# The layout in DRAM of a layer's output and its gradient: by partition and row block instead of row by row

## The chip, the cores and the metric

The kernel runs on one core of a Trainium2 chip. The time is the device time of one execution in microseconds. Before the change three runs took 749.44, 753.18 and 754.14 us; the median is 753.18.

## What is computed

A block with two branches and a gate, forward and backward. For u of 2048 x 448 (L x D) and the output gradient G:

```python
g = sigmoid((u * gate_w).sum(-1, keepdims=True))
a = ssm_conv(u, A, B, C, log_dt) + u * Dskip      # a long convolution, by FFT in the reference
r = relu(u @ w1 + b1)                             # w1: 448 x 1792
b = (r * r) @ w2 + b2                             # w2: 1792 x 448
out = g * a + (1 - g) * b
```

and the gradients of out with respect to u and to all parameters. Everything is bfloat16. For the dense branch (b) the backward pass needs dB = (1 - g) * G, dw2 = (r*r)^T dB, dh = 2 r * (dB w2^T), dw1 = u^T dh, and the part dh w1^T of u's gradient. r and dh have 2048 x 1792 elements, 7.3 MB each.

## The kernel before

The core has 128 partitions. r and dh are held turned: the 1792 columns lie in 14 groups of 128 (`FT = 14`, the index j), one column a partition, with the 2048 rows along the partition. They don't fit into the core's memory beside the convolution's tables, so each group is written to DRAM when it is made (`rT_d` and `dhT_d`, 1792 x 2048 elements, row after row) and read back later. Eight *row blocks* of 256 rows each cut the 2048 rows the other way.

The dense branch is one generator, `dense()`, of 190 or so steps with a hand-written cost for each; the convolution's 14 chunks are the frame, and the steps are put between its parts:

- *First layer* (some 70 to 260 us), for each j: `hidden` makes r's group j by TensorE (L661, L664) and ACT (L676) and stores it (L681 on POOL's queue; the last three, which come while `hold` is set, are deferred and go out on SP's queue, L679). TensorE turns it (L688), ACT squares it (L689), and a product over the rows gives dw2 (L697, stored by L704).
- *Second layer* (some 265 to 450 us), for each j: `load_r` reads group j of r back (L772 whole, or L775 in two halves where j is a multiple of three), three groups ahead; `grad_h` makes dB w2^T (L661, L664), ACT doubles it (L784), and a *gate* on DVE multiplies it by r (L789). The result, dh's group j, is stored by L794 on SP's queue and turned and multiplied by u for dw1.
- *Two projections* (`project`, some 450 to 605 us, the last of it at 630): for each of the eight row blocks, in the order 0, 4, 1, 5, ..., all 14 groups of a block of r are loaded (`load_rows2`, L881 on SP's queue), squared by ACT (L893, the first block L858) and multiplied by w2 (L905); then the same with dh and w1 turned. w1 is turned on its way by a DMA transpose in seven pieces (`load_w1t`, L925, SP's queue). Four buffers take the blocks in turn; three of them get a block in one transfer, the fourth has two pieces of memory and gets it in two transfers of seven groups.

The convolution's chunk c has a table Y that DVE builds in five steps (`build_y`: L1018, L1019, L1021). TensorE multiplies it at once (`kgen`, L1082), and four DMA transposes on SP's queue turn it (`load_yt`, L1106) for chunk c's backward products. The next chunk's first write to Y is a DVE copy, `seeds_y` (L1059), so it waits for those four transposes. The order of the parts in a chunk is written out:

```python
PERIOD = """YS SA Z0 D R Y0 Y1 D Z1 Y2 D R Y3 Z2 D NX Y4 D Z3 KM KO LY WD P0 D P1 D X0 FY0 S FY1 FY2 X1 D R X2 D""".split()
```

YS is `seeds_y`, Y0 to Y4 build Y, KM is `kgen`, LY issues the four transposes, P0 and P1 are DVE's products of the chunk before (L1159, L1161), D lets the dense branch take steps up to a share of its cost. While `hold` is set, transfers that the dense branch wants on SP's queue (r's loads, dh's stores, row blocks, w1's pieces, w2) are put into a list, `held`, by `defer`; R, and LY after its own four transposes, issue what is in the list (`release`). Each engine and each queue runs what it is given strictly in that order.

`rows_of(tensor, j)` at L647 is the address pattern of one group; `load_r` has a pattern of its own for half a group, and `load_rows2` one for a row block. These three are what the diff touches.

Of the kernel before, what the change touches and what calls it, by code (L numbers as in the profile page):

```python
# [19 lines left out]
P = 128  # L20
L, D, N, F = 2048, 448, 256, 1792
LT = L // P
FT = F // P
# [296 lines left out]
def kernel(ctx, tc, A_u, A_A_re, A_A_im, A_B_re, A_B_im, A_C_re, A_C_im, A_log_dt, A_Dskip,  # L320
# [3 lines left out]
    nc = tc.nc  # L324
# [6 lines left out]
    def dscr(name, n, dt=bf16):  # L331
        return nc.dram_tensor(name, (n,), dt, kind="Internal")
# [9 lines left out]
    rT_d = dscr("rT_d", F * L)  # L342
    dhT_d = dscr("dhT_d", F * L)
# [282 lines left out]
    BK = dict(h=("N2", "N3"), t="S", a="X", p=("N0", "N1", "N2", "N3"))  # L626
    dbt, r3, dhs, held, pend = [], [], [], [], []
    hold = False
    db1 = const.tile([P, FT], bf16, name="db1")
    acc = {}  # L630
    rcur, rts = {}, [(b, -1) for b in rt]
# [13 lines left out]
            release()  # L645

    def rows_of(tensor, j):  # L647
        return bass.AP(tensor=tensor, offset=j * P * L, ap=[[L, P], [1, L]])

    def load_w1(jp):  # L650
        b = w1b[jp % 2]
# [15 lines left out]
    def hidden(j, half):  # L667
        pss = wide(half, w1b[j // 2 % 2][:, :, P * (j % 2):P * (j % 2) + P], lambda lb: UT[:, :, 512 * lb:512 * lb + 512])
        if half == 0:
            rcur[j], prev = rts.pop(0)  # L670
            rts.append((rcur[j], j))
            force(prev)
        r = rcur[j]
        for k in range(2):
            lb = 2 * half + k
            S.activation(r[:, 512 * lb:512 * lb + 512], pss[k][:], ACT.Relu, bias=b1_f[:, j:j + 1])  # L676
        if half == 1:
            if hold:
                held.append((j, lambda: nc.sync.dma_start(rows_of(rT_d, j), r)))  # L679
            else:  # L680
                G_.dma_start(rows_of(rT_d, j), r)  # L681
            if j % 2 == 1 and j // 2 + 2 < HP:
                load_w1(j // 2 + 2)
# [37 lines left out]
    def first_layer():  # L721
# [6 lines left out]
        for j in range(FT):  # L728
            if j + 1 < FT:
                hidden(j + 1, 0)  # L730
            turn(j, 0, rcur[j], ACT.Square)
            yield
            if j > 0:
                mul_1(j - 1, 1)
                if j == FT - 3:
                    load_w2(0)
                if j == FT - 1:
                    defer(j, load_u)
                    if r3:
                        load_r(0)  # L740
                        acc["r"] = 1
                yield
            if j + 1 < FT:
                hidden(j + 1, 1)
            turn(j, 1, rcur[j], ACT.Square)
            if j == FT - 2:
                load_w2(1)
            yield
            mul_1(j, 0)
            yield  # L750
            if j in (1, 2):
                for k in range(4):
                    turn_db(4 * j - 4 + k)
                    yield
# [15 lines left out]
    def load_r(j):  # L770
        if j % 3 > 0:
            nc.sync.dma_start(rt[j % 3 - 1], rows_of(rT_d, j))  # L772
        else:
            for h in range(2):
                nc.sync.dma_start(r3[0][h], bass.AP(tensor=rT_d, offset=j * P * L + 1024 * h, ap=[[L, P], [1, 1024]]))  # L775

    def grad_h(j, half):

        force(j - 3)
        pss = wide(half, w2T[j % 2], lambda lb: dbt[lb])  # L780
        dh = dhs[j % 3]
        for k in range(2):
            lb = 2 * half + k
            S.mul(dh[:, 512 * lb:512 * lb + 512], pss[k][:], 2.0)  # L784

        def gate():
            force(j - 3)
            d = dh[:, 1024 * half:1024 * half + 1024]
            V.tensor_tensor(out=d, in0=d, in1=r3[j % 3][half], op=ALU.mult)  # L789
            if half == 1:  # L790
                def go():
                    if j + 3 < FT:
                        load_r(j + 3)
                    nc.sync.dma_start(rows_of(dhT_d, j), dh)  # L794
                defer(j, go)
        pend.append(gate)
# [23 lines left out]
    def second_layer():  # L820

        release()
        for j in range(acc.get("r", 0), 3):
            load_r(j)
# [6 lines left out]
        for j in range(FT):  # L831
            gates()
            if j in (3, 5, 7, 9):
                k0, k1 = (4 * (j // 2) - 4, min(4 * (j // 2), FT))
                defer(j, lambda k0=k0, k1=k1: nc.sync.dma_start(w2n[:, k0:k1], bass.AP(tensor=B_w2.tensor, offset=B_w2.offset + k0 * P * D, ap=[[D, P], [P * D, k1 - k0], [1, D]])))
            if j == FT - 1:
                load_rows2(0)
            if j + 1 < FT:
                grad_h(j + 1, 0)
            turn(j, 0, dhs[j % 3], ACT.Copy)  # L840
            yield
            if j > 0:
                mul_2(j - 1, 1)
            if j + 2 < FT:
                turn_w2(j + 2)
            yield
            gates()
            if j + 1 < FT:
                grad_h(j + 1, 1)
            turn(j, 1, dhs[j % 3], ACT.Copy)  # L850
            yield
            mul_2(j, 0)
            if j > 0:
                turn_back(j - 1)
            yield
# [4 lines left out]
        yield  # L860
        turn_back(FT - 1)
        load_rows2(1)
        defer(98, lambda: load_rows2(2))
        defer(99, lambda: load_rows2(3))
        defer(99, lambda: load_w1t(0))

    PO = [0, 4, 1, 5, 2, 6, 3, 7]
# [5 lines left out]
    def slot_of(n):  # L873

        return pring[0 if n == 15 else n % 4]

    def load_rows2(n):
        bs = slot_of(n)
        m = FT // len(bs)
        for i, b in enumerate(bs):  # L880
            nc.sync.dma_start(b, bass.AP(tensor=rT_d if n < 8 else dhT_d, offset=256 * PO[n % 8] + i * m * P * L, ap=[[L, P], [P * L, m], [1, 256]]))  # L881

    nbk = 0

# [401 lines left out]
    r3 = [[KW[:, 6144:7168], Pt[:, 6144:7168]]] + [[rt[i][:, 0:1024], rt[i][:, 1024:2048]] for i in range(2)]  # L1286
# [105 lines left out]
    i = PERIOD.index("KM")  # L1392
# [303 lines left out]
```

## Time and profile before

The profiled execution took 752.95 us; its span, from the first instruction to the last, is 751.1 us.

| | us | share of the span | instructions |
|---|---|---|---|
| PE (TensorE matmul) | 621.1 | 83% | 8556 |
| DVE (VectorE) | 564.7 | 75% | 932 |
| ACT (ScalarE) | 512.1 | 68% | 873 |
| POOL (GpSimd) | 171.6 | 23% | 296 |

The core moved 177.77 MB in 197,115 DMA packets. SP's queue (q1) had 173,823 of them, 113.11 MB; POOL's (q0) 15,632 and 44.48 MB; ACT's (q10) 7,568 and 18.88 MB. The transfers that touch the two tensors, from the page's list of DMA issues, "us" being the median from issue to landing where the trace has it:

| transfer | line and queue | count | KB each | pieces in DRAM | us |
|---|---|---|---|---|---|
| r's group to rT_d | L681, POOL | 11 | 512 | 4,096 B | 3.0 |
| r's group to rT_d, deferred | L679, SP | 3 | 512 | 4,096 B | |
| r's group back | L772, SP | 9 | 512 | 4,096 B | 4.7 |
| half a group back | L775, SP | 10 | 256 | 2,048 B | 8.8 and 3.1 |
| dh's group to dhT_d | L794, SP | 14 | 512 | 4,096 B | 5.9 |
| row block | L881, SP | 12 | 896 | 512 B | 6.3 to 9.6 |
| half the groups of a row block | L881, SP | 8 | 448 | 512 B | 8.1 |

How to read it: PE, DVE, ACT and POOL are the engines, SP the queue engine that issues most DMAs; "SPq" and "POOLq" are the instructions by which a queue issues. L12 is line 12 of the kernel. An idle time before an instruction stands in brackets with what ended it; a wait for several things is put down to the one that came last by the profile. "PE psN<-D,U" is a matmul that writes psN and reads D and U, buffer numbers left out. A DMA's "share of 16 engines" adds up its packets' times, so it can pass 100% where packets overlap.

### The profile page before, as it was taken

What the parts mean: (1) busy time and instruction counts of PE and PEld (TensorE: products, weight loads), DVE (VectorE), ACT (ScalarE), POOL (GpSimd) and SP (SyncE); (2) the same over time, 40 slices, a digit from 0 to 9 for tenths busy, and PEclk for the clock granted to TensorE, in tenths of its full rate; (3) what the DMA queues carried; (4) which work ended last, traced back from release to release, by engine and by line L of the source; (5) the groups of instructions that cost most, each with busy time, mean ns of one, the idle gap of its engine ahead of it and who ended that gap; (6) DMA issues with size and microseconds to landing.
All of it is one profiled execution on the core that took longest, in us unless ns stands there. A gap on an engine that the chain in (4) does not pass through costs nothing.

```text
span 751.1 us, 20458 instructions
## 1 busy us (share of the span) xinstructions
PE 621.1 (83%) x8556; PEld 337.4 (45%) x8597; DVE 564.7 (75%) x932; ACT 512.1 (68%) x873; POOL 171.6 (23%) x296
## 2 busy tenths in 40 slices
PE   5947968779999787999989997888969978687666
PEld 2412323323346453665665664555545664433111
DVE  1495586675698456899898997988699877959473
ACT  2895958587887576778777777777634535597555
POOL 2251112111263220211201201110100332411543
PEclk9887967879999899999999999999989988799758
DMA  9997586827773997997997989999999966998995
GB/s 211 220 280 243 195 294 240 291 103 285 283 263 134 249 256 214 200 249 203 219 209 216 240 137 240 244 198 245 218 186 234 276 165 199 389 333 297 333 327 147
DMA packets 197115, 177.77 MB, mean 237 GB/s; under 512 B 121534, under 2 KB 174039, under 8 KB 196895
## 3 DMA queue, kind: packets, MB, share of 16 engines
q1 hardware_dynamic: 173823, 113.11, 61.9%
q0 software_dynamic: 15632, 44.48, 19.3%
q10 hardware_dynamic: 7568, 18.88, 6.7%
q8 instruction: 67, 1.10, 0.6%
q14 instruction: 25, 0.20, 0.1%
HBM read 83.95 MB, written 64.32 MB: 197 GB/s over the span
## 4 chain that ended last, share of the span: by engine, by line
PE 28%; DMA 12%; DVE 10%; ACT 7%; issue 7%; POOL 1%; SPq 0%; POOLq 0%; ACTq 0%; DVEq 0%
PE psN L905 5%; PE psS L1176 5%; DMA R<-Y 3%; PE psN L661 3%; PE psX L1082 3%; PE psN L697 3%; DVE Y L1021 2%; DVE Y L1018 2%; DVE F L1019 2%; DMA U<-in_A_u_dram 2%; DMA S<-in_B_w_dram 2%; DMA hd<-F 2%; PE psN L296 1%; PE psF L1144 1%; ACT P L1150 1%
## 5 line engine op out<-in xcount | busy, mean ns | idle before, releaser
L697 PEld LDWEIGHTS <-U 128*128 128x128 bf16 x448 | 40.6, 99 | 42.4 <-issue 12.1
L1150 ACT CAST P<-psF 128x1024 bf16<-128x1024 f32 x52 | 53.1, 1021 | 7.0 <-PE psF L1144 6.8
L1018 DVE TENSOR_TENSOR Y<-Y,F 128x1024 bf16<-128x1024 bf16 (+3 forms) x70 | 48.0, 686 | 2.7
L661 PEld LDWEIGHTS <-S 128*128 128x128 bf16 x336 | 30.2, 101 | 44.1 <-issue 18.5
L1021 DVE TENSOR_TENSOR Y<-Y,F 128x1024 bf16<-128x1024 bf16 (+3 forms) x70 | 48.1, 687 | 2.4
L697 PE MATMUL psN<-S,U 128*128 128x449 bf16 x224 | 47.8, 355 | 0.2 <-issue 0.2
L661 PE MATMUL psN<-S 128*128 128x512 bf16 x153 | 46.3, 415 | 1.9 <-issue 1.0
L1019 DVE TENSOR_TENSOR F<-Y,F 128x1024 bf16<-128x1024 bf16 (+3 forms) x70 | 47.2, 674 | 0.0
L697 PE MATMUL psX<-D,U 128*128 128x448 bf16 x160 | 37.3, 370 | 2.0 <-ACT D L703 2.0
L689 ACT ACTIVATE U<-psN 128x1024 bf16<-128x1024 bf16 x35 | 36.1, 1032 | 1.5 <-PE psN L688 1.5
L1183 POOL DMA_DIRECT2D s_d<-st x28 | 14.0, 506 | 97.6 <-ACT st L1181 97.6
L905 PEld LDWEIGHTS <-U 128*128 128x128 bf16 x252 | 24.2, 100 | 24.7 <-issue 4.7
L676 ACT ACTIVATE U<-psN,b_f 128x512 bf16<-128x512 f32 x48 | 31.0, 688 | 6.0 <-PE psN L664 4.3
L1144 PEld LDWEIGHTS <-R 41*128 41x128 bf16 x1792 | 27.0, 93 | 17.8 <-issue 15.0
L1144 PE MATMUL psF<-S,R 41*128 41x32 bf16 x1664 | 29.4, 174 | 5.9 <-ACT P L1150 5.9
L661 PE MATMUL psN<-K,S 128*128 128x512 bf16 x100 | 27.6, 391 | 5.6 <-issue 3.2
L905 PE MATMUL psN<-S,U 128*128 128x448 bf16 x140 | 29.0, 358 | 1.8 <-DMA S<-in_B_w_dram 1.8
L296 PEld LDWEIGHTS <-cb_MI 64*128 64x128 bf16 x256 | 15.6, 98 | 32.1 <-issue 23.6
L1176 PE MATMUL psS<-ident,P 128*64 128x128 bf16 x896 | 27.4, 219 | 0.0
L1176 PEld LDWEIGHTS <-M 128*64 128x64 bf16 x896 | 25.7, 110 | 3.0 <-issue 1.5
L1059 DVE COPY Y<-rec 128x256 bf16<-128x256 bf16 x14 | 10.6, 755 | 21.5 <-DMA R<-Y 15.5
L1176 PEld LDWEIGHTS <-P 128*64 128x64 bf16 x896 | 25.9, 110 | 0.0
(417 smaller groups left out, 1688.7 us busy)
## 6 DMA issues: line engine op xcount, KB each, us to landing
sp<-K ACTq DMA_DIRECT2D x8, 896.0 KB, 4.2
rT_d<-U POOLq DMA_DIRECT2D x11, 512.0 KB, 3.0
hd<-F SPq DMA_DIRECT2D x11, 448.0 KB, 14.1
U<-rT_d SPq DMA_DIRECT2D x9, 512.0 KB, 4.7
X<-gd SPq DMA_DIRECT2D x5, 896.0 KB
U<-dhT_d SPq DMA_DIRECT2D x5, 896.0 KB, 9.6
rec_d<-F ACTq DMA_DIRECT2D x2, 1920.0 KB
hd<-st ACTq DMA_DIRECT2D x8, 448.0 KB, 4.8
```

The lines of the kernel that those rows point to most:

```text
L296: nc.tensor.matmul(ps[kk2][:, 0:D], lhsT=m[r0:r0 + 64], rhs=x[r0:r0 + 64, 2 * q2 + ii, ri, :], start=(k == 0), stop=(k == len(terms) - 1), ...
L661: T_.matmul(pss[k][:], lhsT=w[:, dt], rhs=x(2 * half + k)[:, dt], start=(dt == 0), stop=False, skip_group_check=True)
L676: S.activation(r[:, 512 * lb:512 * lb + 512], pss[k][:], ACT.Relu, bias=b1_f[:, j:j + 1])
L689: S.activation(hn[j % 2][:, 8 * th:8 * th + 8, :], ps[:], f)
L697: T_.matmul(ps[:, 0:w], lhsT=hn[j % 2][:, t, :], rhs=rhs[:, t, :], start=(t == 0), stop=(t == LT - 1))
L905: T_.matmul(ps[:, 0:D], lhsT=src[j][:, P * x:P * x + P], rhs=ws[:, j, :], start=(j == 0), stop=(j == FT - 1))
L1018: V.tensor_tensor(out=run(yb, dst, [64, X2], [d0[1], n // d0[1]], [1, d0[1]]), in0=run(yb, 0, [64, X2], *src), in1=pr, op=ALU.mult)
L1019: V.tensor_tensor(out=run(vb, 0, [n, X2], [d0[1], n // d0[1]], [1, d0[1]]), in0=run(yb, 0, [64, X2], *src), in1=pi, op=ALU.mult)
L1021: return V.tensor_tensor(out=hi, in0=hi, in1=run(vb, n, [2 * n, W2], [-n, 2], [1, n]), op=ALU.add)
L1144: T_.matmul(psz[t][:, 32 * b:32 * b + 32], lhsT=yt[64 * t:64 * t + NY, b, :], rhs=DKc[64 * t:64 * t + NY, c % 2, 16 * (j % 2) + b].rearran ...
L1150: S.copy(run(zbs[c, h][:, 0:1], 16 * (j % 2), [1024, 2], [64, NA], [32, 2], [1, 16]), run(psF[:, 0, 0:1], 0, [512, 2], [1, NA], [NA, 2], [ ...
L1176: T_.matmul(sps[64 * h:64 * h + 64, cc, r, :], lhsT=Q[h][r][:, 1024 * t + 64 * a:1024 * t + 64 * a + 64], rhs=(nident if r == 0 and t == 1 ...
```

## The change

Both tensors are laid out with the partition slowest, then the row block, then the group, then the row in the block: partition p has 8 x 14 x 256 elements in one piece of 57,344 bytes, and a row block of one partition is 14 x 256 elements, 7,168 bytes, in one piece. A group of one partition is now eight pieces of 512 bytes instead of one of 4,096; half a group is four of 512 instead of one of 2,048. The number of transfers, the bytes that each moves and the order in which they are issued are the same, and the places in the core's memory too.

```diff
@@ in the dense branch's set-up
     hold = False
+    HW = 256 * FT
@@ the address pattern of one group, for the stores (L679, L681, L794) and the whole loads (L772)
     def rows_of(tensor, j):
-        return bass.AP(tensor=tensor, offset=j * P * L, ap=[[L, P], [1, L]])
+        return bass.AP(tensor=tensor, offset=256 * j, ap=[[8 * HW, P], [HW, 8], [1, 256]])
@@ load_r, half a group (L775)
             for h in range(2):
-                nc.sync.dma_start(r3[0][h], bass.AP(tensor=rT_d, offset=j * P * L + 1024 * h, ap=[[L, P], [1, 1024]]))
+                nc.sync.dma_start(r3[0][h], bass.AP(tensor=rT_d, offset=256 * j + 4 * h * HW, ap=[[8 * HW, P], [HW, 4], [1, 256]]))
@@ load_rows2, a row block (L881)
         for i, b in enumerate(bs):
-            nc.sync.dma_start(b, bass.AP(tensor=rT_d if n < 8 else dhT_d, offset=256 * PO[n % 8] + i * m * P * L, ap=[[L, P], [P * L, m], [1, 256]]))
+            nc.sync.dma_start(b, bass.AP(tensor=rT_d if n < 8 else dhT_d, offset=HW * PO[n % 8] + i * 256 * m, ap=[[8 * HW, P], [1, 256 * m]]))
```

`P` is 128, `L` 2048, `FT` 14, `PO` the order of the row blocks, `bs` the pieces of memory of the buffer and `m` the groups that go into each (14 or 7).

## The prediction

> **What bounds the kernel now.** The profiled execution took 752.95 us, its span 751.1, so 1.85 us lie around the span; the median of the three runs is 753.18, and the sums below are made against 752.95. I read the windows of the four stages first, then the chain of waits between 450 and 605 us, then the timelines of SP and DVE around the places where the chain leaves the engines for a DMA, and last the DMA traffic in short windows with one kind of transfer in them.
>
> The windows (engine busy time, then clock, DMA share of 16 engines, GB/s):
> ```profile
> 70.00:250.00 180.00, 152.37 (x1181) 68.35 (x1192) 130.77 (x246) 135.78 (x237) 45.20 (x64) 0.89 0.63 226
> 265.00:450.00 185.00, 169.49 (x3216) 109.08 (x3241) 159.31 (x226) 137.40 (x239) 28.80 (x52) 0.98 0.95 213
> 450.00:605.00 155.00, 134.68 (x2647) 85.56 (x2647) 131.39 (x185) 96.29 (x136) 22.94 (x41) 0.95 1.09 234
> ```
> First layer, second layer, the two projections. TensorE is busy 92% of the second layer; in the projections the DMA engines are never free (1.09, overlapping packets counted twice), and both engines have 13 to 15% idle. There the chain of waits runs in a ring: the steps that build Y on DVE (L1018 to L1021), then the four DMA transposes that read Y (L1106), then the DVE copy that overwrites Y for the next chunk (L1059). DVE, 488 to 541 us:
> ```profile
> 491.11 0.69 DVE L1021 TENSOR_TENSOR Y<-Y,F 128x1024 bf16<-128x1024 bf16 x1
> 509.20 0.74 DVE L1059 COPY Y<-rec 128x256 bf16<-128x256 bf16 x1 [2.94 <-DMA R<-Y]
> ...
> 519.70 0.69 DVE L1021 TENSOR_TENSOR Y<-Y,F 128x1024 bf16<-128x1024 bf16 x1
> 540.25 0.74 DVE L1059 COPY Y<-rec 128x256 bf16<-128x256 bf16 x1 [7.01 <-DMA R<-Y]
> ```
> DVE stood 2.94 and 7.01 us until the transposes had read Y. SP's queue shows what stood before them:
> ```profile
> 488.95 0.51 SPq L881 DMA_DIRECT2D U<-rT_d  x1
> 489.50 3.34 SPq L925 DMA_TRANSPOSE S<-in_B_w_dram  x1
> 492.94 12.65 SPq L1106 DMA_TRANSPOSE R<-Y  x4
> ...
> 515.88 1.40 SPq L881 DMA_DIRECT2D U<-dhT_d  x1
> 517.32 4.45 SPq L925 DMA_TRANSPOSE S<-in_B_w_dram  x1
> 521.87 13.73 SPq L1106 DMA_TRANSPOSE R<-Y  x4
> ```
> Y was ready at 491.80 and 520.39, but SP was still issuing an L925 transpose, behind a row-block load, until 492.84 and 521.77: the four started 1.1 and 1.5 us late, and the load's data lay ahead of theirs. The third set in this stage, issued at 551.91 with nothing outstanding ahead of it, ran 13.1 us to its DVE copy (565.05); these two ran 16.3 and 18.4.
>
> The price of a piece size, in windows of one kind: row-block loads now (512 B pieces), 7,168 B pieces, row stores now (4,096 B pieces), and a POOL store of 512 B pieces (DBT_d, L711, where POOL puts eight in a 4,096 B packet):
> ```profile
> DMA packets 1142, 0.58 MB, mean 292 GB/s; under 512 B 0, under 2 KB 1142, under 8 KB 1142
> ```
> ```profile
> DMA packets 55, 0.39 MB, mean 394 GB/s; under 512 B 0, under 2 KB 0, under 8 KB 55
> ```
> ```profile
> DMA packets 218, 0.80 MB, mean 399 GB/s; under 512 B 23, under 2 KB 23, under 8 KB 218
> ```
> ```profile
> DMA packets 35, 0.14 MB, mean 287 GB/s; under 512 B 0, under 2 KB 0, under 8 KB 35
> ```
> (544 to 546, 593 to 594, 272.5 to 274.5, 143 to 143.5 us.) So 512 B pieces move at 290 GB/s whichever way they go, long ones at 394 to 400.
>
> **The change part by part.** Instructions, their order on every engine and what they wait for stay; only the shapes of 67 transfers change, and no arithmetic.
>
> *The row-block loads* (L881): 16 blocks in 20 transfers, 917,504 B a block. 3.14 us at 292 GB/s become 2.33 at 394: 0.8 a block, 13 us in all, within 450 to 605.
>
> *The row transfers*: 28 stores of 524,288 B (L681 x11, L679 x3, L794 x14) and 14 loads of the same size (L772 x9, L775 x5 pairs) go from 4,096 or 2,048 B pieces to 512 B. 1.31 us become 1.81: +0.5 each, +0.25 a half, 21 us in all. No store of 512 B pieces from SP's queue is in the trace; the DBT_d row is the nearest, and 169 GB/s (279 to 285 us, the slowest stretch of small pieces) bounds it from above: 3.1 us, +1.8 a store. Below zero I see no row. I take +0.5.
>
> The DMA engines thus get 8 us more work, but it counts only where somebody waits.
>
> *First layer.* 11 stores on POOL, +0.5 us of data each where the engines are 63% busy. POOL's issue: 0.542 us at 128 pieces, 0.714 for L711 at 512, so 0.45 ns a piece and 0.94 us at 1,024. Behind a store on POOL stand the w1 loads and the out_12 stores; POOL is 25% busy there and nobody waits for L681. Should the cover fail, the buffer is wanted back by L676 some ten us later, against landings of 3.0 us now and 5.9 for L711. I take +0.3 (0 to 2).
>
> *Start of the second layer.* Here the DMA engines are busy almost without a gap from 269 to 292 us, and DVE waits for a row load:
> ```profile
> 292.04 0.69 DVE L789 TENSOR_TENSOR F<-F,U 128x1024 bf16<-128x1024 bf16 x1 [4.10 <-DMA U<-rT_d]
> ```
> Ahead of it on SP, since 269: two half loads, three deferred stores, two loads of u; then it. 2 x 0.25 + 3 x 0.5 + 0.5 = 2.5 us later. Y's steps stand behind this gate on DVE, the transposes at 300.90 start as Y ends, and TensorE's L1082 came only 0.6 us after Y: that is all the slack. +2.2 (1 to 3).
>
> *The rest of the second layer.* Of the six sets of transposes from 300 to 450 us two have row transfers issued within 4 us before them (a half load and a store at 325.05 and 325.46 ahead of 328.94; a load and a store at 351.70 and 352.11 ahead of 355.59): 0.75 and 1.0 us, exposed, as DVE waited up to 2.7 us for the transposes there. One transpose takes 1.8 to 4.8 us to issue (median 3.0), which may swallow part. +0.9 (0 to 1.8). The other four have 7 us or more of empty queue before them. Loads of r are issued 15 us and more before their gates; 0.5 us there is hidden by that, and would cost itself if it weren't.
>
> *The projections.* 492.94: the load ahead is 0.8 us shorter and SP free up to 1.1 us sooner; DVE's 2.94 us wait covers it: -1.7 (-0.8 to -1.9). 521.87: the three loads ahead (505.69 to 515.88) are 2.4 us shorter together, SP free 1.4 us sooner; -2.4 (-1 to -4), covered by 7.01. What is late next is TensorE, which itself waited 1.56 and 5.71 us for Y at 520.45 and 551.93, so it follows. Sets 461.96, 551.91, 576.00: Y's end met a free SP, nothing (0 to -0.8 together). ACT's squares waited 1.81 us for a block at 481.26; DVE was not behind it: -0.3 (0 to -0.9).
>
> Sum: 0.3 + 2.2 + 0.9 - 1.7 - 2.4 - 0.3 = -1.0, so 752.95 - 1.0 = 752.0. With all bounds against it: 2 + 3 + 1.8 - 0.8 - 1 = +5, 758; all for it: 1 - 1.9 - 4 - 0.8 - 0.9 = -6.6, 746.
>
> [...]
>
> **The rivals.**
>
> *Pieces of 512 B cost no more than long ones*, or all of it is hidden: nothing moves, 753. For it: no engine waits for most of these transfers. Against: 292 beside 394 GB/s. [...]
>
> *Faster: SP comes free.* The seven L925 transposes, 229 KB each, hold SP 27.9 us together (6.20, 4.91, 4.45 the longest), behind 512 B loads, while a 512 KB one (L1106) issues in 3.0 in the median. If short queues of pieces are what frees SP, both late sets fall to the 13.1 us of the third: -3.2 and -5.3, with late starts of 1.1 and 1.5 gone, -11, capped by DVE's 2.94 + 7.01 at -10; with 0.3 + 2.2 of cost, -7.5: 745. Against: the set at 300.90, with nothing issued ahead of it for 15 us, ran 16.3 us all the same.
>
> *Slower: SP's stores of 512 B pieces write at the slow rate*, 169 GB/s: +1.8 each. Then the start of the second layer pays 3 x 1.8 + 1.0 = 6.4, the two exposed sets 0.25 + 1.8 + 0.5 + 1.8 = 4.3, and the last stores (448.12 and 451.35), ahead of the first block load, nothing to 2, taken as 1; with the first layer's 0.3 it is 12.0, less the gain of 4.4: +7.6, 761. Five stores lie on the path, so the sign turns from +0.7 a store on, and 1% is reached at +1.8. For it: no such store is in the trace. Against: 287 GB/s into DRAM at the same piece size.
>
> That the change doesn't reach the hardware is no case: the built program has loads of 128 x 3584 and stores of 1024 x 256 elements.
>
> **How the numbers follow.** Forecast 0.57, no cost of pieces 0.09, faster 0.16, slower 0.18. A measurement here can tell about 1%, 7.5 us. The forecast's own bounds (746 to 758) and the second case lie within it; the third (1.0%) and the fourth (1.1%) lie just at it and are counted whole as faster and slower. So same 0.66, faster 0.16, slower 0.18. The range takes both outer cases in: 744 to 762.
>
> **What would show it.** Right: 450 to 605 us shorter by 3 to 5 us, L1059 waits at the second and third set of it down to some 1 and 4.5 us, L925's issues shorter; L789's wait of 4.10 at 6 to 7; row stores at 290 GB/s. Wrong: row stores well under 290 GB/s, or sets of transposes in the second layer that start behind stores more than twice; or sets in the projections that stay at 16 to 18 us with the loads out of their way, which would mean that POOL's traffic, not these loads, made them long.

## The result, and the profile after the change

The changed kernel takes 757.31 us (median of 11 runs, 752.82 to 763.04) against 752.21 (11 runs, 748.61 to 755.37) on the same chip: a ratio of 1.0070, 95% interval 1.0041 to 1.0099 (the ratios here leave out runs more than 1.5% above a kernel's fastest: above all three of e4_r's twelve below, and in the last batch eight of the seventeen of the kernel before and six of g_late2048's twelve). It is 5 us slower where the forecast had it 1 us faster (752.0). Its profiled execution took 757.5 us with a span of 755.7, 4.6 more than the span of before.

**Along the way the profile looks much as forecast.** The windows of the three stages (length, then PE, PEld, DVE, ACT and POOL busy with instruction counts, clock, DMA share, GB/s):

```profile
70.00:250.00 180.00, 151.47 (x1120) 68.00 (x1130) 129.55 (x245) 136.22 (x238) 49.01 (x64) 0.90 0.65 226
265.00:450.00 185.00, 168.28 (x3231) 108.67 (x3252) 157.00 (x224) 136.95 (x237) 29.44 (x53) 0.98 0.99 213
450.00:605.00 155.00, 135.84 (x2692) 86.76 (x2687) 135.52 (x187) 99.25 (x143) 22.48 (x39) 0.98 1.01 240
```

The DMA share rose by 0.02 and 0.04 in the two layers, where the rows are stored and read in short pieces, and fell by 0.08 in the projections, where they are read in long ones. POOL is busy 3.8 us longer in the first layer: eleven issues of 0.87 us (median) instead of 0.54. (The lines after the diff have moved down by one: L1059 of before is L1060 here.)

The gate that waited 4.10 us for a row load, and the copies that wait for the second and third set of transposes, in DVE's timeline:

```profile
294.92 0.69 DVE L790 TENSOR_TENSOR F<-F,U 128x1024 bf16<-128x1024 bf16 x1 [5.48 <-DMA U<-rT_d]
...
507.91 0.99 DVE L1060 COPY Y<-rec 128x256 bf16<-128x256 bf16 x1 [0.86 <-DMA R<-Y]
...
538.28 0.74 DVE L1060 COPY Y<-rec 128x256 bf16<-128x256 bf16 x1 [5.88 <-DMA R<-Y]
```

The gate is 2.9 us later than before (292.04), and its wait 1.4 longer. The copy of the second set waits 0.86 us instead of 2.94; that of the third 5.88 instead of 7.01. SP's queue ahead of those two sets:

```profile
485.73 0.51 SPq L882 DMA_DIRECT2D U<-rT_d  x1
486.28 4.56 SPq L926 DMA_TRANSPOSE S<-in_B_w_dram  x1
492.31 11.51 SPq L1107 DMA_TRANSPOSE R<-Y  x4
...
512.22 0.54 SPq L882 DMA_DIRECT2D U<-dhT_d  x1
512.81 5.62 SPq L926 DMA_TRANSPOSE S<-in_B_w_dram  x1
519.38 13.88 SPq L1107 DMA_TRANSPOSE R<-Y  x4
```

SP is now free at 490.84 and 518.43, before the last step of Y (L1022 at 491.60 and 518.66, 0.69 us each), and both sets start when Y ends. And the prices of the pieces, the DMA traffic from 274 to 276 us (the deferred stores of r, in 512 B pieces) and from 541 to 542 (row-block loads of 7,168 B pieces):

```profile
DMA packets 1281, 0.65 MB, mean 323 GB/s; under 512 B 20, under 2 KB 1281, under 8 KB 1281
```
```profile
DMA packets 59, 0.42 MB, mean 423 GB/s; under 512 B 0, under 2 KB 0, under 8 KB 59
```

**The loss lies behind all of this.** The last compute instructions and the last data are where they were: the chain of waits ends with POOL's store L1660 at 745.67 us (745.74 before), and the last packets of data move at 748.4 in both. The end of that chain, before and after:

```profile
745.74 0.51 POOL out_dram L1659
746.25 0.51 POOLq L1691
```
```profile
745.67 0.52 POOL out_dram L1660
746.19 0.50 POOLq L1692
```

What follows is POOL's DRAIN. Every engine has drains on the program's last line, and the last ones of all other engines come only when POOL's long one has ended: at 750.6 and 750.7 us before, where it ends at 750.4, and at 755.2 and 755.3 after, where it ends at 754.9. The instructions of the program's last line, before and after (engine, kind, count: shortest/median/longest in ns, start of the first and of the last):

```profile
L1691 POOLq DRAIN  x3: 46/108/4187, 746.2 to 750.9; - x3
L1691 SPq DRAIN  x3: 7/7/13, 749.2 to 750.6; - x3
```
```profile
L1692 POOLq DRAIN  x3: 46/107/8833, 746.1 to 755.5; - x3
L1692 SPq DRAIN  x3: 7/7/13, 749.1 to 755.2; - x3
L1692 ACTq EVENT_SEMAPHORE  x2: 17/17/17, 755.1 to 755.7; - x2
L1692 DVEq EVENT_SEMAPHORE  x2: 21/21/21, 755.1 to 755.7; - x2
```

POOL's long drain starts at 746.2 us before and at 746.1 after, and takes 8.83 us instead of 4.19, +4.65. SP had issued its last store by 747.5, and its own drains take 7 to 13 ns. The last data moved 2.3 us into POOL's drain; the DMA traffic from 748.6 to 754.9 us is

```profile
DMA packets 0, 0.00 MB, mean 0 GB/s; under 512 B 0, under 2 KB 0, under 8 KB 0
```

ACT's and DVE's last semaphores come at 755.1 to 755.7, when POOL's drain has ended (754.9). The views of busy time don't show this: they have POOL 0.00 us busy from 747.0 to 754.9, in the midst of its drain, and the chain of waits only ends with "POOLq L1692" and a length of 0.50.

### The profile page after: what moved, and what is told of

Its sections match the earlier page's. It is cut to its first block, busy times and chain, and to the rows that moved or that the text cites. A ratio compares the mean times of both kernels' runs of the same rounds, so it can differ in the third digit from the quotient of the medians.

```text
span 755.7 us, 20458 instructions
## 1 busy us (share of the span) xinstructions
PE 614.7 (81%) x8556; PEld 335.3 (44%) x8597; DVE 566.2 (75%) x932; ACT 511.6 (68%) x873; POOL 176.1 (23%) x296
## 3 DMA queue, kind: packets, MB, share of 16 engines
q0 software_dynamic: 15632, 44.48, 19.2%
## 5 line engine op out<-in xcount | busy, mean ns | idle before, releaser
L1022 DVE TENSOR_TENSOR Y<-Y,F 128x1024 bf16<-128x1024 bf16 (+3 forms) x70 | 48.1, 687 | 2.4
L236 PEld LDWEIGHTS <-cb_F1BD 128*128 128x128 bf16 x96 | 9.8, 108 | 35.5 <-issue 26.8
```

The costliest lines, as they stand in the source:

```text
L1022: return V.tensor_tensor(out=hi, in0=hi, in1=run(vb, n, [2 * n, W2], [-n, 2], [1, n]), op=ALU.add)
```

## The experiments

**First batch: is it the number of pieces, and whose?** By the destinations of its transfers in the trace, POOL issued 42,935 pieces before and 52,791 after, though its queue moved 15,632 packets and 44.48 MB in both. Theory A was that each adds 0.47 ns to the drain; B, that the drain is a chance and the loss lies in SP's stores; C, that pieces cost at the end on whatever queue. e1_act has `nc.scalar` where e1_sp has `nc.sync`, e2_dose1 one extra transfer where e2_dose3 has three; `dum_d` is a DRAM tensor that nobody reads.

```diff
 e1_sp: the changed kernel, L682
-                G_.dma_start(rows_of(rT_d, j), r)
+                nc.sync.dma_start(rows_of(rT_d, j), r)
 e2_dose3: the kernel before, behind L681
                 G_.dma_start(rows_of(rT_d, j), r)
+                for x in range(3):
+                    G_.dma_start(bass.AP(tensor=dum_d, offset=(3 * j + x) * P * 384, ap=[[384, P], [48, 8], [1, 32]]), r[:, 0:256])
```

> The changed kernel, but the 11 stores of L681 are issued by SP instead of POOL; their 1,024 pieces each stay. Theory A (POOL's last drain grows by some 0.47 ns with every piece that POOL has issued: 4.64 us for 9,856 more pieces): POOL now issues 11 x 128 = 1,408 pieces fewer than before the change, so its last drain takes 3.5 to 4.2 us, against 8.83 in the changed kernel, and the whole takes 752 us, 5 less than the changed kernel and 0 to 1 less than before. Theory B (the drain's 8.83 us is a chance of one execution, and the loss comes from the 512 B stores and loads on SP's queue in the second layer): 757 us or more, since SP now has eleven such stores more. Theory C (pieces cost at the end whichever queue issues them): the time stays at 757, with the 4.6 us in another engine's last drain.

> The changed kernel, but the 11 stores of L681 are issued by ACT, which makes r, instead of POOL. Theory A: POOL's last drain 3.5 to 4.2 us; 752 us, plus what 11 issues cost ACT in the first layer, where it is busy 136 of 180 us: 0 to 3. Theory B: 757 or more. Theory C: 757, the 4.6 us in ACT's last drain.

> The kernel before, with one extra transfer on POOL behind each of the 11 stores of L681: 64 KB in 1,024 pieces of 64 B, into a DRAM tensor that nobody reads; 11,264 pieces more, 0.7 MB, and no change to the layout. Theory A: POOL's last drain 4.19 + 11,264 x 0.47 ns = 9.5 us, the time 5.3 us above before. Theory B: the drain stays at 4.2 and the time within 1 us of before.

> The same with three extra transfers behind each store, 33,792 pieces more. If the drain grows with the sum of the pieces without end (theory A): 4.19 + 15.9 = 20 us, the time 16 us above before and up to 3 more where POOL's queue, 31 us busier in the first layer, makes somebody wait. If what the drain works off is a ring of 32,768 pieces (A2; by the shapes in the trace POOL issues some 42,900 pieces before and 52,800 after the change; less 32,768 these are 10,200 and 20,000, which at 0.41 and 0.44 ns give the two drains 4.19 and 8.83): it stays near 4.7 us, the time 0 to 3 above before. Theory B: 4.2 us.

| kernel | pieces against before | drain, us | ratio to before (95%) |
|---|---|---|---|
| e1_sp | -1,408 | 9.24 | 1.0109 (1.0059 to 1.0158) |
| e1_act | -1,408 | 9.24 | 1.0237 (1.0182 to 1.0291) |
| e2_dose1 | +11,264 | 9.07 | 1.0068 (1.0038 to 1.0099) |
| e2_dose3 | +33,792 | 4.26 | 1.0035 (0.9999 to 1.0071) |

e1_sp is 8 us slower than before, of which its drain makes 5.05. All three theories fall: A by e1_sp, whose drain is longer with fewer pieces; B by e2_dose1, where the drain and the time go up without any change of the layout; C because no other engine's last drain grew (ACT's longest is 779 ns in e1_act and after the change, 776 before it). The ring of 32,768 pieces (A2) came near for e2_dose3 (4.7 expected), but it would give e1_sp 3.6 us. The lines of e1_sp, with fewer pieces on POOL than before, of e2_dose1, and of e2_dose3, with the most of all:

```profile
L1692 POOLq DRAIN  x3: 46/108/9237, 748.0 to 757.8; - x3
```
```profile
L1694 POOLq DRAIN  x3: 46/107/9073, 748.7 to 758.3; - x3
```
```profile
L1694 POOLq DRAIN  x3: 46/108/4255, 744.7 to 749.5; - x3
```

The drain is not a sum over pieces, but it is no chance either: e1_sp and e1_act issue the same transfers on POOL, and their drains are 9,237 ns both, though one starts at 748.0 and the other at 757.9 us. (ACT as the issuer cost the first layer some 13 us by itself: the first set of transposes starts at 270.0 us there, at 256.9 in the changed kernel.) So in these runs the drain went with what POOL's queue had been given, and not in one direction (4.19 us before, 9.07 with one extra transfer a store, 4.26 with three). My guess from this was something that starts over.

**Second batch: a ring?** Theory R, a guess from the five different drains so far: the drain depends on where the count stands in a ring of 16,384 pieces. The same extra transfer, in other numbers:

```diff
 d1_after7: the changed kernel, L682 (d3_before7 the same in the kernel before, d2_before4 with 4 for 7)
                 G_.dma_start(rows_of(rT_d, j), r)
+                if j < 7:
+                    G_.dma_start(bass.AP(tensor=dum_d, offset=j * P * 384, ap=[[384, P], [48, 8], [1, 32]]), r[:, 0:256])
 e3_dh: the changed kernel, with rT_d stored and read as before
     def rows_of(tensor, j):
+        if tensor is rT_d:
+            return bass.AP(tensor=tensor, offset=j * P * L, ap=[[L, P], [1, L]])
```

In e3_dh the loads of half a group (L776) and of r's row blocks (L882, n < 8) have the patterns of before too.

> The changed kernel with 7 extra transfers on POOL, one behind each of the first seven stores of L681: 64 KB in 1,024 pieces of 64 B each, into a DRAM tensor that nobody reads. Theory R (the last drain of POOL depends on where the count of the pieces that POOL issued stands in a ring of 16,384; counted from the kernel before, the five positions seen are 0: 4.19, 1,024: 4.26, 9,856: 8.83, 11,264: 9.07 and 14,976: 9.24 us): the position is 9,856 + 7,168 - 16,384 = 640, so the drain falls to 4.2 us although POOL does more, and the time falls by 4.6 us below the changed kernel's, to about that of before. Theory A (every piece adds 0.47 ns): 12.2 us, the time 3.4 above the changed kernel's. Theory B (each program has a value of its own by chance): any of the two values, 4.2 or 9.

> The kernel before with 4 such extra transfers, 4,096 pieces: position 4,096. Theory R with a straight line between the positions seen (1,024: 4.26 and 9,856: 8.83): 5.8 us. Theory R with a step between two values: 4.3, or 8.7 if the step comes before 4,096. Theory A: 6.1.

> The kernel before with 7 such extra transfers, 7,168 pieces: position 7,168. Theory R with a straight line: 7.4 us. With a step between two values: 4.3 or 8.8. Theory A: 7.6.

> The changed layout for dh alone; r is stored and read as before the change. POOL's queue is then that of the kernel before, so theory R expects a drain of 4.19 us; so does A. The three deferred stores and the loads of r at the start of the second layer are as before (the +2.2 of the prediction gone), the 14 stores of dh have 512 B pieces (+0.9 at most), and the eight blocks of dh in the projections are loaded in long pieces (about two thirds of the -4.4 of the prediction, as the two loads next to the set at 521.87 are dh's and one of r's): 752.2 + 0.9 - 2.5 = 750.6, 0.2% below before. If instead the second layer's stores of 512 B pieces are what costs, it is above before.

Measured: d1_after7 7.61 us and a ratio of 1.0065 (1.0033 to 1.0098); d2_before4 6.46 and d3_before7 7.69, in one run each (5.8 and 7.4 by R with a straight line); e3_dh 4.19 and 1.0007 (0.9976 to 1.0038). A fell for good: d1_after7, with the changed kernel's transfers and seven more, has a shorter drain than the changed kernel's 8.83. The lines of d1_after7 and of e3_dh:

```profile
L1695 POOLq DRAIN  x3: 46/108/7607, 751.3 to 759.5; - x3
```
```profile
L1697 POOLq DRAIN  x3: 46/108/4192, 751.7 to 756.4; - x3
```

But R in this form missed as well (it had 4.2 us there). e3_dh's time is level with before where 0.2% less was expected; its interval holds both. Its drain, with a POOL queue like that of the kernel before, is within 5 ns of it: 4,192 against 4,187.

With eight drains in hand a better rule could be sought (R2): POOL's transfers are counted, each as a sixteenth of its pieces plus one, and where the next transfer would take the count past a fixed size, it starts again with that transfer. The expectations call this a ring and its units entries; no trace shows either, and the sixteenth and the one were assumed. As an estimate from the eight drains and the pieces of POOL's transfers in the traces, a size of 744, the only thing fitted, puts all but the two largest of the eight in order (9.24 us stands at 700, 9.07 at 733), and the drain goes with the *number of transfers* since the last start, or with what they count.

**Third batch: does the estimate foretell?** One extra transfer on POOL, near the end, in three sizes (f_late1024 has 8 pieces of 8 elements a partition, f_late3072 24 of 4):

```diff
 f_late2048: the changed kernel, behind the last stores of out_0
+    G_.dma_start(bass.AP(tensor=dum_d, offset=0, ap=[[768, P], [32, 16], [1, 8]]), ident[:, 0:128])
     close(3)
 e4_r: the changed kernel, with dhT_d stored and read as before
```

> The changed kernel with one extra transfer on POOL near the end, behind the last stores of out_0 (10 transfers of POOL's queue follow): 1,024 pieces of 16 B from ident into a DRAM tensor that nobody reads. The eight drains measured so far can be put in order by one rule, whose size was fitted to them (theory R2): POOL's queue fills a ring of some 744 entries an engine, each transfer taking a sixteenth of its pieces plus one; a transfer that doesn't fit in what is left starts again at the front; and the last drain grows with what stands in the ring since it last started at the front: 60 entries (13 transfers) 4.19 us, 316 (49) 6.46, 445 (66) 7.61, 472 (69) 7.69, 634 (79) 8.83, 700 (81) 9.24, 733 (82) 9.07. The changed kernel ends at 634; 65 more make 699: R2 expects about 9.2 us. Theory A (each piece 0.47 ns): 9.3. Theory B (a value of its own for each program): anything from 4 to 9.

> The same with 2,048 pieces: 634 + 129 entries pass 744 a few transfers before the end, so the ring starts again there. R2: the drain falls to 4.2 us or a little less, and the time to 752.5 to 753 us, 0.6% below the changed kernel's and level with before, with one transfer more than the changed kernel. Theory A: 9.8 us. Theory B: anything.

> The same with 3,072 pieces: the extra transfer itself (193 entries) doesn't fit and starts the ring again, and ten transfers follow. If the number of transfers in the ring sets the drain: 11 of them, about 4.1 us. If the entries set it: 250 of them, about 5.9. Theory A: 10.3.

> The changed layout for r alone; dh is stored and read as before the change. POOL's queue is that of the changed kernel, so every theory of POOL's queue expects its 8.83 us of drain, 4.6 more than before. Along the way: the start of the second layer as in the changed kernel (+2 to +3 at the sets of transposes of 300 to 360 us), no 512 B stores of dh (-0.5 or so of that), and of the projections' gain what r's blocks bring (-1.7 at the set of 492.94 and a third of the -2.4 at 521.87): 752.2 + 4.6 + 2.2 - 2.5 = 756.5. If the loss sits in dh's stores instead of the drain: 752 or less.

The drains of f_late1024, f_late2048 and f_late3072:

```profile
L1694 POOLq DRAIN  x3: 46/108/8910, 743.3 to 752.7; - x3
```
```profile
L1694 POOLq DRAIN  x3: 46/108/3016, 745.3 to 748.9; - x3
```
```profile
L1694 POOLq DRAIN  x3: 46/108/3562, 758.4 to 762.5; - x3
```

8.91, then 3.02, then 3.56 us, for 1,024, 2,048 and 3,072 pieces: as R2 had it, to 1.2 us at worst (f_late2048, below the "4.2 or a little less"). The transfer of 1,024 pieces added 0.08 us to the changed kernel's 8.83; the one of 2,048, after which by R2 the count starts again, took 5.8 us away. The last tells the two apart: by R2 the count stands at some 240 but 11 transfers have come since the last start, and the drain is 3.56, not 5.9. As an estimate from all drains measured so far, 2.96 us + 74 ns for each transfer since the last start fits to 0.4 us; with another number than one added to the sixteenth (0 to 5), or with a count that runs on over its size, no size of 100 to 2,100 fits to better than 1.6 us:

| kernels | transfers since the last start, by R2 | drain by the estimate, us | drain measured, us |
|---|---|---|---|
| f_late2048 | 6 | 3.40 | 3.02 |
| f_late3072 | 11 | 3.77 | 3.56 |
| before, e3_dh | 13 | 3.92 | 4.19, 4.19 |
| e2_dose3 | 13 | 3.92 | 4.26 |
| d2_before4 | 49 | 6.59 | 6.46 |
| d1_after7, d3_before7 | 66, 69 | 7.84, 8.07 | 7.61, 7.69 |
| after, e4_r | 79 | 8.81 | 8.83, 8.83 |
| f_late1024 | 80 | 8.88 | 8.91 |
| e1_sp, e1_act | 81 | 8.95 | 9.24, 9.24 |
| e2_dose1 | 82 | 9.03 | 9.07 |

The time followed for f_late2048: 0.9965 of before (0.9933 to 0.9997), with the whole change in it and one useless transfer more. e4_r's drain was the changed kernel's (8.83), but its time is hard to read: twelve runs from 749.46 to 764.47 us with a median of 758.67 against 755.69 of before, and yet a ratio of 0.9991 (0.9950 to 1.0032). f_late1024 and f_late3072 ran once each, and their times say nothing of the drain: 754.77 us with the long one and 764.50 with the short one. The lines above show why: the drain starts at 743.3 us in the first and at 758.4 in the second, so what one execution takes up to the drain scatters more than the drains differ.

**Fourth batch: is the drain the whole difference?** The changed kernel and f_late2048 on one chip, and the kernel before with its drain first raised (as in e2_dose1) and then cut by a late transfer:

```diff
 g_bdose: e2_dose1, behind the last stores of out_0
+    G_.dma_start(bass.AP(tensor=dum_d, offset=11 * P * 384, ap=[[768, P], [32, 16], [1, 8]]), ident[:, 0:128])
```

> The changed kernel again. Rule R2 (2.96 us plus 74 ns for each transfer in POOL's ring since it last started at the front): the drain is 8.83 us as before, to some hundredths. If the drain is the whole of the difference, the time is 4.6 us (0.6%) above before; with the forecast's -1.0 along the way 3.6 (0.5%).

> The changed kernel with the one extra transfer of 2,048 pieces near its end, again. R2: the drain is 3.02 us as in the first run, 5.8 less than the changed kernel's: 1.2 us below before where the layout by itself gives nothing, 2.2 (0.3%) with the forecast's -1.0. If the layout costs 2 us along the way, as the mean distances between the sets of transposes in the profiles have it: 0.8 above before.

> The kernel before with the 11 extra transfers of the first dose (drain 9.07 us, 0.68% above before) and one more transfer on POOL, 2,048 pieces of 16 B, behind the last stores of out_0. R2: that transfer doesn't fit in the ring any more and 10 follow it, so the drain falls from 9.07 to 3.6 us, and the time from 0.7% above before to 0.1% below it (-0.6 us). Theory A (each piece 0.47 ns): 10 us and 0.8% above.

The drains:

```profile
L1692 POOLq DRAIN  x3: 46/108/8828, 749.8 to 759.1; - x3
```
```profile
L1694 POOLq DRAIN  x3: 46/108/2958, 750.9 to 754.5; - x3
```
```profile
L1695 POOLq DRAIN  x3: 46/108/3078, 752.2 to 755.9; - x3
```

They came out at 8.83, 2.96 and 3.08 us, the first two within 60 ns of their first runs; g_bdose's is shorter than the 3.6 expected, the largest miss of the estimate (3.77, 0.7 us too high). The times scattered more than in any other batch, before's from 743.27 to 764.13. g_after 1.0159 (1.0075 to 1.0242), median 760.37; g_late2048 0.9983 (0.9922 to 1.0044), median 752.25; the median of before 754.41. So the same program with one transfer more was some 8 us faster by the medians, 5.9 of which are the drain's. g_bdose at 1.0103 (1.0023 to 1.0182), median 756.30, did not follow its drain; why, beyond this batch's scatter, stays open.

Set beside the kernel before of the same batch by the medians of all runs, the kernels that ran more than once differ from it by what their drains differ, to 2.0 us; g_bdose is 3.0 us longer than that, and e1_act 10.5 (its first layer).

## Why the prediction was wrong, step by step

**The step that failed** is the term of the first layer's stores on POOL: "POOL is 25% busy there and nobody waits for L681", "+0.3 (0 to 2)". The issue price was near (0.87 us measured, 0.94 forecast), and no wait shows in the first layer: the first set of transposes starts at 255 to 259 us with the old layout and at 252 to 259 with the new one (the profiles of the table below). But the end of the program waits: the drain went from 4.19 to 8.83 us, +4.65, where the profiled spans differ by 4.6. The change gave those eleven transfers 1,024 pieces each instead of 128; by R2, an estimate from the drains of the experiments, that moves the last start from 13 to 79 transfers before the end. The sum ended at the last data; I did not look at what lies between that and the end of the span, though the chain of waits named POOL there. One trace would not have led to R2, but it shows the 4.19 us that POOL keeps the program open, of which 1.9 come after the last data.

**The other steps** need more than two profiles, since single executions of one layout differ by 2 us and more at any place (2.1 to 9.1 us in the ranges below). So I took the starts of the sets of transposes in SP's timelines of all profiles: six with the rows laid out as before (before, d2_before4, d3_before7, e2_dose1, e2_dose3, g_bdose), eight as after (after, g_after, e1_sp, d1_after7, f_late1024, f_late2048, g_late2048, f_late3072). Mean distances in us, with the ranges:

| stretch | old layout | new layout | difference | forecast |
|---|---|---|---|---|
| first to second set (255 to 301 us in before) | 45.1 (42.7 to 46.2) | 47.9 (46.9 to 49.0) | +2.8 | +2.2 |
| second to eighth (to 462) | 160.2 (158.5 to 161.7) | 161.3 (158.6 to 164.1) | +1.1 | +0.9 |
| eighth to ninth (to 493) | 31.5 (31.0 to 33.3) | 29.5 (27.7 to 31.4) | -2.0 | -1.7 - 0.3 |
| ninth to eleventh (to 552) | 58.6 (57.1 to 60.3) | 58.1 (53.5 to 62.6) | -0.6 | -2.4 |

- *Start of the second layer*: right, and the ranges don't overlap. It is r's layout: e4_r (r new, dh old) has 48.96, e3_dh (dh new, r old) 45.93. That the three deferred stores and the loads ahead make it is as the order in SP's queue has it; they were not tried apart.
- *Rest of the second layer*: the mean is as forecast, but the ranges cover each other.
- *Set 492.94*: right. e4_r has 29.82, e3_dh 31.50: it is r's loads.
- *Set 521.87*: mostly wrong. SP came free and the set started with Y, but the gain was given back inside it: from its start to its DVE copy 18.9 us in the profile of after, 18.4 before. In after 96 of the 128 pieces of the dh block ahead moved in the first 4 us after the set's start, 0.69 MB; before it was 771 pieces of 512 B, 0.39 MB. Freeing the issuer let the set start sooner behind data that still had to move. This is read from the traces, not tested. The prediction had named a set that stays this long as a sign that POOL's traffic makes it so; 0.49 MB of that moves in the set with either layout, from 530 us on in after, and its part was not tried.
- *Prices*: 512 B stores of SP run at 323 GB/s, not 290, so a store costs +0.3 us rather than +0.5; long loads at 423 (394 forecast). The seven L926 issues sum to 23.8 us (27.9 before).

The sum of the table is +1.3, against -1.3 forecast for the same rows; the times say as little: f_late2048's and g_late2048's ratios, less the 1.2 us by which their drains are shorter than before's, leave -1.4 and -0.1 us for the layout, each plus or minus 2.4 us or more. Whether the layout by itself gains or loses one microsecond stays open. The drain is what decided the sign: with the layout kept and the drain shortened by one transfer, neither f_late2048 nor g_late2048 is measurably slower than before.

**The rivals.** That 512 B pieces cost nothing is refuted by the first row of the table. "SP comes free" gave shorter issues but not the time, for the reason under the set 521.87. "SP's stores write at the slow rate" is refuted by the 323 GB/s: the result has the sign of this rival, and not its mechanism.

## What to carry to other kernels

Add up a change to the end of the span, not to the last data: read how long the last drain of each engine is, POOL's above all, and ask what the change gives that engine's queue. In this kernel POOL's drain took 3.0 to 9.2 us, and edits of POOL's transfers moved it in either direction: from 4.19 to 9.07 us with one extra transfer behind each of the eleven stores of the first layer, and to 4.26 with three; from 8.83 to 3.02 with one extra transfer near the end. When two layouts are compared, compare them at equal drains: here one useless transfer of 2,048 pieces near the end made the changed kernel level with before or 0.35% better, at a drain 1.2 us shorter than before's.

## What the runs showed that was not expected

- With the same transfers on its queue POOL's drain at the end of the program came out alike, to 5 ns in three cases and 58 ns in a fourth: 9,237 and 9,237 ns; 4,187 and 4,192; 8,833, 8,832 and 8,828; 3,016 and 2,958.
- It was shorter with more work: 3.02 us with 54,839 pieces issued, 8.83 with 52,791, and 9.24 with 41,527.
- R2 (a count that starts again at 744, and about 3 us + 74 ns for each transfer since) is an estimate, fitted to the drains of twelve different queues, of which the last four were foretold, all too high: by 0.3, up to 1.2, 0.5 and 0.5 us. No trace shows what is counted, and what POOL does in that time isn't visible: in the profile of after no data moves past the first 2.3 of the drain's 8.83 us.
